# Sliding-window attention on TensorE as dense 128 by 136 score tiles per head, in place of elementwise work on VectorE and the weaving of two token classes

## The chip, the cores and the metric

The kernel runs on one core of a Trainium2 chip. The metric is the time on the device in microseconds, lower is better. The spread of one kernel's runs is small: the kernel before took 1353.09 to 1357.71 us. The mean granted TensorE clock of the profiled run was 0.989 for the kernel before.

The engines go by these names: PE is TensorE (matmuls), PEld its weight loads, DVE is VectorE, ACT is ScalarE, POOL is GpSimd, SP issues the DMAs.

## The reference, cut to what matters

Four blocks in a row, attention, MLP, attention, MLP, over 2048 tokens of width 1024, in bf16. The attention looks back at eight tokens, two apart: token s sees s, s-2, ..., s-14. So even and odd tokens never meet in it, and they form two "classes" of 1024 tokens each. There are 32 heads of 32 dimensions. The MLP mixes tokens: its first product contracts over all 2048 tokens, both classes.

```python
def _A_ref(x, wqkv, wo):              # H = 32, Dh = 32, W = 8, dil = 2
    qkv = ... (x @ wqkv) ...          # B, H, S, Dh each
    off = jnp.arange(W) * dil
    idx = pos[:, None] - off[None, :]
    mask = idx >= 0
    logits = jnp.einsum("bhsd,bhswd->bhsw", q, kg) * scale     # kg = k gathered at idx
    logits = jnp.where(mask[None, None, :, :], logits, -1e9)
    attn = _softmax(logits, axis=-1)
    o = jnp.einsum("bhsw,bhswd->bhsd", attn, vg)
    return (...o...) @ wo

def _B_ref(x, w1, b1, w2, b2):        # F = 3584
    h = _layernorm(x)
    u = _gelu(jnp.einsum("bsd,sf->bdf", h, w1) + b1)
    y = jnp.einsum("bdf,fs->bds", u, w2) + b2
    return y.transpose(...)

x = x + _A_ref(_layernorm(x), A_wqkv, A_wo);  x = x + _B_ref(_layernorm(x), ...)    # twice
```

## The kernel before

Tokens lie on the partitions: partition p holds eight tokens of a class that follow each other. A query and its eight keys then lie on one partition, apart from a halo of seven slots that two DMAs fetch from the partition above. Scores and values are elementwise work of DVE on chunks of eight heads (`QW` is 256), with tree sums over the 32 dimensions; in three chunks the sums run on PE as products with the identity.

```python
def qk(self, ci):                                   # scores of one chunk, on DVE
    ...                                             # three chunks: tree sums by identity matmuls on PE
    for u0 in range(0, W, WB):                      # WB = 2 of the 8 offsets at a time
        nc.vector.tensor_tensor(out=flat, in0=qb, in1=windows(k, u0, WB, [(1, J * QW)]), op=ALU.mult)
        nc.vector.tensor_tensor(out=pr[:, :, 0:16, :], in0=pr[:, :, 0:16, :], in1=pr[:, :, 16:32, :], op=ALU.add)
        nc.vector.tensor_tensor(out=pr[:, :, 0:8, :], in0=pr[:, :, 0:8, :], in1=pr[:, :, 8:16, :], op=ALU.add)
        nc.vector.tensor_tensor(out=St[...], in0=pr[:, :, 0:4, :], in1=pr[:, :, 4:8, :], op=ALU.add)
...
def pv(self, ci):                                   # values, on DVE
    for u in range(W):
        dst = Tv if u else o_q
        nc.vector.tensor_tensor(out=dst[...], in0=v, in1=pw, op=ALU.mult)
        if u:
            nc.vector.tensor_tensor(out=o_q[:], in0=o_q[:], in1=Tv[:], op=ALU.add)
    self.transpose(ci, 0, J)                        # a DMA transpose for the output projection
...
def proj(self, ci, *parts, ...):                    # Q, K or V of a chunk: 256-column matmuls
    for jp in range(J // 2):
        for part in parts:
            ...
            nc.tensor.matmul(ps[:, jj, :], lhsT=self.lhs(c, kt, j), rhs=wts[part][:, kt, :], ...)
            nc.scalar.activation(out=buf[...], in_=ps[...], func=ACT.Identity)      # ACT empties PSUM
            ...                                     # halo DMAs for K and V
```

While DVE works at a chunk, a generator called `weave` hands PE other matmuls, by declared costs of each piece: the output projection of the other class, partial sums of the first MLP product over one class, or the second MLP product of the layer before for the second class.

```python
for unit in chain(lead, last):                      # lead: the attention stream; fill: other matmuls
    ...
    add(unit)
    while t[0] < t[1]:                              # t = [PE time, DVE time] by declared costs
        u = next(fill, None)
        if u is None:
            break
        add(u)
```

## Time and profile before

| what | before |
|---|---|
| time, median | 1355.73 us (later runs beside it: 1355.34) |
| span of the profiled run | 1353.0 us |
| PE busy | 1294.1 us, 96% |
| DVE busy | 772.2 us, 57% |
| ACT busy | 434.4 us, 32% |

The page of the kernel before, its first and fourth parts and three lines of its fifth. In the first, each engine has its busy time, share of the span and number of instructions. In the fourth, shares of the chain of waits that ended last. In the fifth, a group's line, engine and operation, its shapes, its count, then busy us, mean ns of one, and the engine's idle time before it.

```profile
span 1353.0 us, 18269 instructions
...
PE 1294.1 (96%) x7552; PEld 759.6 (56%) x7552; DVE 772.2 (57%) x959; ACT 434.4 (32%) x884; POOL 40.5 (3%) x28
...
PE 59%; DVE 27%; issue 6%; ACT 3%; DMA 2%; POOL 2%; SPq 0%; POOLq 0%; DVEq 0%; ACTq 0%
...
L272 PE MATMUL ps<-wq,hT 128*128 128x256 bf16 x3008 | 351.4, 277 | 21.4 <-ACT v L274 12.9
...
L308 DVE TENSOR_TENSOR T<-q,k 128x4096 bf16<-128x4096 bf16 x52 | 118.6, 2281 | 37.1 <-ACT q L274 23.1
```

The mean of one 256-column matmul is 277 ns, but that is latency: matmuls follow each other faster than they finish. The Trainium skill, "Trainium Kernel Development and Optimization", Performance Expectations, warns of this: it calls matmul busy time a bad metric, because matmuls are pipelined. These matmuls are 277 ns long, but start 109 ns apart. What counts is the cadence, from start to start, and the chain of waits shows it. Here are two pieces of it for the kernel before (start in us, length in us, what):

```profile
228.51 3.49 PE ps L272 x32
...
498.11 6.04 PE pso L559 x28
```

So 32 matmuls of 256 columns take 3.49 us, 0.109 us each, and 28 of 512 columns take 6.04 us, 0.2158 us each (0.1092 and 0.21583 before rounding, which the table uses). With the counts of the groups PE has this dense work:

| PE work before | matmuls | us |
|---|---|---|
| two MLP products, both layers | 3584 of 512 columns | 773.5 |
| output projection | 512 of 512 | 110.5 |
| Q, K, V | 3072 of 256 | 335.4 |
| identity matmuls (tree sums, value sums, residual) | 320 | 48.6 |
| transposes of the first tiles | 64 of 128 | 3.6 |
| sum | | 1271.6 |

The span is 1353.0 us. The first matmul starts at 7.7 us and the last ends 4.4 us before the end. Some 69 us are left.

The view of waits says what PE waited for; these are its largest entries before a matmul (waiter, what it waited for, us in total, times, longest):

```profile
PE ps L272 <- ACT v L274: 12.9, 8, 2.8
...
PE pso L236 <- DVE g L211: 8.2, 2, 7.7
...
PE pso L375 <- DVE T L372: 7.0, 1, 7.0
PE pso L559 <- DMA w<-in_B_w_dram: 6.2, 3, 2.3
```

### The profile page before, as it was taken

What the parts mean: (1) busy time and instruction counts of PE and PEld (TensorE: products, weight loads), DVE (VectorE), ACT (ScalarE), POOL (GpSimd) and SP (SyncE); (2) the same over time, 40 slices, a digit from 0 to 9 for tenths busy, and PEclk for the clock granted to TensorE, in tenths of its full rate; (3) what the DMA queues carried; (4) which work ended last, traced back from release to release, by engine and by line L of the source; (5) the groups of instructions that cost most, each with busy time, mean ns of one, the idle gap of its engine ahead of it and who ended that gap; (6) DMA issues with size and microseconds to landing.
All of it is one profiled execution on the core that took longest, in us unless ns stands there. A gap on an engine that the chain in (4) does not pass through costs nothing.

```text
span 1353.0 us, 18269 instructions
## 1 busy us (share of the span) xinstructions
PE 1294.1 (96%) x7552; PEld 759.6 (56%) x7552; DVE 772.2 (57%) x959; ACT 434.4 (32%) x884; POOL 40.5 (3%) x28
## 2 busy tenths in 40 slices
PE   6989999999999999999998999989799999999998
PEld 5877756754444444459674488665344444444443
DVE  4899999996711433327999649979761033111111
ACT  4377347533122430003333434763222134000000
POOL 2000000000000000000000000100000000000000
PEclk9999999999999999999999999999899999999999
DMA  4458543743452229864477954444245222434431
GB/s 126 149 121 187 139 115 121 191 108 94 133 140 78 74 73 224 223 166 127 138 176 188 233 161 117 140 135 109 71 136 142 64 85 67 119 96 116 137 101 59
DMA packets 290111, 175.18 MB, mean 129 GB/s; under 512 B 66445, under 2 KB 267657, under 8 KB 290026
## 3 DMA queue, kind: packets, MB, share of 16 engines
q1 hardware_dynamic: 289914, 173.98, 48.1%
q8 instruction: 59, 0.97, 0.3%
q14 instruction: 26, 0.21, 0.1%
q0 software_dynamic: 112, 0.01, 0.0%
HBM read 127.94 MB, written 16.78 MB: 107 GB/s over the span
## 4 chain that ended last, share of the span: by engine, by line
PE 59%; DVE 27%; issue 6%; ACT 3%; DMA 2%; POOL 2%; SPq 0%; POOLq 0%; DVEq 0%; ACTq 0%
PE psg L537 13%; PE psg L559 11%; PE pso L559 11%; PE pso L537 8%; DVE Tv L356 6%; PE ps L272 6%; DVE o_q L359 5%; DVE T L308 5%; PE pso L503 5%; PE ps L537 4%; DVE T L310 2%; DVE T L293 1%; POOL L L326 1%; DVE T L312 1%; DVE St L314 1%
## 5 line engine op out<-in xcount | busy, mean ns | idle before, releaser
L272 PE MATMUL ps<-wq,hT 128*128 128x256 bf16 x3008 | 351.4, 277 | 21.4 <-ACT v L274 12.9
L272 PEld LDWEIGHTS <-hT 128*128 128x128 bf16 x3072 | 323.3, 122 | 55.6 <-issue 17.4
L559 PEld LDWEIGHTS <-w 128*128 128x128 bf16 x1792 | 174.9, 98 | 217.3 <-DMA w<-in_B_w_dram 9.3
L537 PEld LDWEIGHTS <-w 128*128 128x128 bf16 x1792 | 175.8, 98 | 212.7 <-issue 4.8
L537 PE MATMUL psg<-h,w 128*128 128x512 bf16 x896 | 211.1, 381 | 0.0
L559 PE MATMUL pso<-g,w 128*128 128x512 bf16 x896 | 199.9, 379 | 6.3 <-DMA w<-in_B_w_dram 6.2
L559 PE MATMUL psg<-g,w 128*128 128x512 bf16 x896 | 198.9, 379 | 0.0
L537 PE MATMUL pso<-h,w 128*128 128x512 bf16 x640 | 151.5, 379 | 1.9 <-ACT h L216 1.9
L308 DVE TENSOR_TENSOR T<-q,k 128x4096 bf16<-128x4096 bf16 x52 | 118.6, 2281 | 37.1 <-ACT q L274 23.1
L503 PE MATMUL pso<-wo,oT 128*128 128x512 bf16 x512 | 118.6, 381 | 3.5 <-DMA oT<-o_q 3.4
L548 DVE TENSOR_TENSOR tmp<-pso,g 128x512 f32<-128x512 f32 x40 | 27.7, 692 | 159.4 <-PE pso L537 159.4
L359 DVE TENSOR_TENSOR o_q<-o_q,Tv 128x2048 bf16<-128x2048 bf16 x91 | 111.2, 1222 | 0.8
L356 DVE TENSOR_TENSOR Tv<-v,Pb 128x2048 bf16<-128x2048 bf16 x91 | 110.8, 1218 | 0.7
L564 DVE SCALAR_TENSOR_TENSOR xo<-psg,b_sb,xs 128x512 bf16<-128x512 f32 x32 | 24.0, 749 | 127.0 <-PE psg L559 127.0
L564 DVE SCALAR_TENSOR_TENSOR xo<-pso,b_sb,xs 128x512 bf16<-128x512 f32 x32 | 24.0, 749 | 120.3 <-PE pso L559 112.4
L503 PEld LDWEIGHTS <-oT 128*128 128x128 bf16 x512 | 50.1, 98 | 63.1 <-DMA oT<-o_q 4.2
L549 ACT ACTIVATE g<-tmp,b_sb 128x512 bf16<-128x512 f32 x80 | 57.7, 721 | 82.1 <-DVE tmp L548 82.1
L310 DVE TENSOR_TENSOR T<-T 128x2048 bf16<-128x2048 bf16 x52 | 63.1, 1214 | 0.4
L274 ACT ACTIVATE k<-ps 128x512 bf16<-128x512 f32 x64 | 38.1, 596 | 69.7 <-PE ps L272 67.7
L178 ACT ACTIVATE ln<-mv,eps 128x1 f32<-128x1 f32 x32 | 9.5, 296 | 152.9 <-DVE mv L187 152.9
L326 POOL TENSOR_SCALAR_AFFINE_SELECT L<-L 1x512 f32<-1x512 f32 x16 | 31.2, 1949 | 910.5 <-DVE L L323 815.7
L537 PE MATMUL ps<-h,w 128*128 128x512 bf16 x256 | 57.9, 379 | 0.0
(89 smaller groups left out, 831.4 us busy)
## 6 DMA issues: line engine op xcount, KB each, us to landing
w<-in_B_w_dram SPq DMA_DIRECT2D x96, 448.0 KB, 4.6
w<-in_B_w_dram SPq DMA_DIRECT2D x56, 512.0 KB, 5.1
wq<-in_A_wqkv_dram SPq DMA_DIRECT2D x47, 512.0 KB, 4.3
wo<-in_A_wo_dram SPq DMA_DIRECT2D x64, 128.0 KB, 2.8
xa<-xn SPq DMA_DIRECT2D x32, 256.0 KB, 2.1
xs<-xa SPq DMA_DIRECT2D x32, 256.0 KB, 3.3
v<-v SPq DMA_DIRECT2D x16, 392.0 KB, 4.9
k<-k SPq DMA_DIRECT2D x15, 392.0 KB, 5.1
```

The source lines that it names most:

```text
L272: nc.tensor.matmul(ps[:, jj, :], lhsT=self.lhs(c, kt, j), rhs=wts[part][:, kt, :], start=(kt == 0), stop=(kt == KD - 1))
L274: nc.scalar.activation(out=buf[:, off + 2 * jp:off + 2 * jp + 2, :].rearrange("p j (d h) -> p j d h", h=HQ), in_=ps[:].rearrange("p j (h d ...
L308: nc.vector.tensor_tensor(out=flat, in0=qb, in1=windows(k, u0, WB, [(1, J * QW)]), op=ALU.mult)
L310: nc.vector.tensor_tensor(out=pr[:, :, 0:16, :], in0=pr[:, :, 0:16, :], in1=pr[:, :, 16:32, :], op=ALU.add)
L326: nc.gpsimd.affine_select(out=L[0:1], in_=L[0:1], compare_op=ALU.is_ge, fill=NEG, base=1 - W, pattern=[[1, W], [1, J], [0, HQ]], channel_m ...
L356: nc.vector.tensor_tensor(out=dst[:].rearrange("p j (d h) -> p j d h", h=HQ), in0=v, in1=pw, op=ALU.mult)
L359: nc.vector.tensor_tensor(out=o_q[:], in0=o_q[:], in1=Tv[:], op=ALU.add)
L503: nc.tensor.matmul(ps[:], lhsT=at_.oT[c][kt // 2][:, j, kt % 2, :], rhs=wo_t[n][kt // 4][:, kt % 4, :], start=(kt == 0), stop=(kt == KD - ...
L537: nc.tensor.matmul(ps[:], lhsT=wt[c][:, j, fl * P:(fl + 1) * P], rhs=h2[c][:, j, dc * 512:(dc + 1) * 512], start=(k == 0), stop=(k == nk - 1))
L549: nc.scalar.activation(out=gs, in_=tmp[:], func=ACT.Gelu_apprx_tanh, bias=b1_sb[:, ft:ft + 1])
L559: nc.tensor.matmul(ps[:], lhsT=w2t[ft // HF][:, ft % HF, c::DIL], rhs=g[ft // GF][:, ft % GF, dc * 512:(dc + 1) * 512], start=(ft == 0), s ...
L564: nc.vector.scalar_tensor_tensor(out=xo[:, dc * 512:(dc + 1) * 512], in0=ps[:], scalar=b2_sb[:, i, c:c + 1], in1=xs[:, dc * 512:(dc + 1) * ...
```

## The change

The intent is to give attention to PE. The heads now lie on the partitions (`qT`, `kT`: four heads of 32 dimensions make 128 rows). For a tile of 128 keys and one head, one matmul computes the scores of these keys against 136 queries (128 and the 8 that follow, since the window reaches seven back in the class). It has 32 rows, so four heads use the four 32-row tiles of the array. ACT takes the exp (with a constant shift, no maximum), DVE multiplies by a band of ones and zeros, and PE multiplies by V, 32 columns a head, so that four heads use the four 32-column tiles. Matmuls with ones give the denominators; Ln and Exp on ACT turn them into reciprocals. No class has to wait for the other, and the weave, the halo copies and the partial MLP sums go. The diff, cut to its core:

```diff
-    def qk(self, ci): ...          # elementwise scores on DVE, 52 products of 4096 elements
-    def softmax(self): ...
-    def pv(self, ci): ...          # 104 products and 91 sums of 2048 elements on DVE
-    def pv_pe(self, ci, bufs): ... # value sums by identity matmuls
-    def weave(lead, fill, then, last): ...
+    def qk_chunk(u, wts, part, n):             # 8 matmuls of 512 columns: Q or K of 4 heads, 512 tokens
+        ...
+        nc.vector.tensor_copy(out=dst[:, lo:lo + 512], in_=ps[:])
+    def scores(u, r):                          # round r: 3, 3 or 2 tiles of 128 keys, 4 heads
+        ss = [s_tile() for _ in range(2)]
+        for t in ts:
+            lo = c * SC + t * P
+            for h in range(HG):
+                hp = slice(h * DH, (h + 1) * DH)
+                nc.tensor.matmul(ss[h // 2][:, h % 2, (t - ts[0]) * KW:(t - ts[0] + 1) * KW],
+                                 lhsT=k[hp, lo:lo + P], rhs=q[hp, lo:lo + KW], start=True, stop=True)
+        for b in range(2):
+            pv = pm[:, 2 * b:2 * b + 2, ts[0]:ts[0] + n, :]
+            nc.scalar.activation(out=..., in_=ss[b][:, :, 0:n * KW], func=ACT.Exp, scale=scale, bias=shift[:])
+            nc.vector.tensor_tensor(out=pv, in0=pv, in1=mk, op=ALU.mult)          # band mask
+    def values(u, b, v, oT):                   # half b: 4 tiles of 128 tokens
+        acc = a_tile()                         # one buffer, 2 x 512 columns in fp32
+        for i in range(-1 if b else 0, hb):
+            for h in range(HG):
+                ... nc.tensor.matmul(acc[hp, 0, ...], lhsT=lhs, rhs=pm[:, h, t, 0:w], ...)
+        for h in range(HG):
+            ... nc.tensor.matmul(acc[hp, 1, :]..., lhsT=ones[:], rhs=pm[:, h, t0:t0 + hb, 0:P], ...)
+        ...                                    # and the 8 columns that reach over: ones again
+        nc.scalar.activation(out=rd[:], in_=acc[:, 1, :], func=ACT.Ln)
+        nc.scalar.activation(out=rd[:], in_=rd[:], func=ACT.Exp, scale=-1.0)
+        nc.vector.tensor_tensor(out=oT[g][:, lo:lo + hb * P], in0=acc[:, 0, :], in1=rd[:], op=ALU.mult)
+    for u in range(NU):                        # 16 units a layer: 4 heads, one class
+        ...                                    # fill: the four projection chunks of the next unit
+        scores(u, 0)
+        fill[0]()
+        if u:
+            values(u - 1, 1, v, oT)
+        scores(u, 1)
+        fill[1]()
+        scores(u, 2)
+        fill[2]()
+        values(u, 0, v, oT)
+        fill[3]()
```

## The prediction

> **What bounds the kernel now.** TensorE. The page's first part gives PE 1294.1 us busy (96% of 1353.0 us), DVE 772.2 (57%), ACT 434.4. PE busy counts latency, so I cost it by cadence. The chain of waits shows 28 matmuls of 512 columns in 6.04 us (0.2158 us each); 128 projection matmuls of 256 columns take 13.96 us (0.109 each). With the groups' counts: MLP 3584 x 0.2158 = 773 us, output projection 512 x 0.2158 = 110, QKV 3072 x 0.109 = 335, identity matmuls and transposes about 52. Sum 1271. So about 82 us are PE slack: the start, and attention, where DVE holds the chain (27% of it; a q*k product takes 2.28 us).
>
> **Removed.** DVE attention: q*k products and tree sums (about 240 us), value products and sums (about 270), softmax pieces (about 100); halo copies; partial first-GEMM sums and their 80 adds; most of the 52 us of identity matmuls.
>
> **Unchanged.** MLP and output projection on PE, 884 us. QKV becomes 1536 matmuls of 512 columns: 331 us, the same. Dense PE work is 1217 us; the rest must fit in 136 us to tie.
>
> **Added**, per unit (4 heads, one class; 32 units). On PE 32 score matmuls of 136 columns on 32-row tiles, 36 value matmuls (mostly 136 columns) and 16 with ones on 32-column tiles. End to end at the cadence above that is near 5.8 us; if four tiles run together, near 1.6. The Trainium skill, "TensorEngine Tiling (Array Packing)", Key Properties, says that tiles execute in parallel and that changing the tiling mode drains the engine; no run shows either. The built order has about 12 mode changes a unit; my guess is 0.1 us each. I take 2.0 us for matmuls plus 1.0 for changes.
>
> ACT per unit: exp of 816 elements x4 and 544 x2, Ln and Exp of 512 x2. From a 512-element copy at 0.59 us and 1024 at 1.01: 0.84, 0.61 and 0.6, together 7.0 us. DVE: band mask (2048 elements 1.22 us, 512 0.42, so 816 about 0.58) 3.2 us, four copies out of PSUM 2.7, two products 1.4: 7.3 us. PE has 6.9 us of projection per unit plus 3, so PE leads, but both score buffers serve each round: the third round waits for the second's two exps behind Ln and Exp. I allow 0.5 us. A unit then takes 10.4 us, against 6.9 of projection.
>
> **Sum.** 1217 dense + about 18 start + 4 tail + 8 stage changes + 32 x 3.3 = 1353. I predict **1350 us, 1305 to 1415**. Faster by over 2%: 0.30; within 2%: 0.40; slower by over 2%: 0.30. The freed DVE time can return at most the 82 us of slack, and the new PE work takes about that back.
>
> **What would show it.** DVE busy falls to 350-430 us, ACT rises to about 420. A middle unit lasts 10 to 11 us. Four score matmuls of different row tiles start within about 60 to 120 ns if tiles overlap, about 230 if not. Chain of waits: nearly all PE, with ACT exp and DVE mask pieces in attention.
>
> **What would make it wrong.** No tile overlap: a unit of 13 to 14 us, above 1440. Near-free mode changes and full overlap: a unit of 8.8, near 1300. Exp, Ln and mask latencies serialising with the single value accumulator: 12 us, 1400. A slow start through twelve DMA transposes: 10 us more.

(One reading in it was taken at one remove: the 13.96 us for 128 projection matmuls is four times the 3.49 us for 32 shown above.)

## The result, and the profile after

| what | before | after |
|---|---|---|
| time, median | 1355.34 us (4 runs) | 1340.16 us (4 runs) |
| ratio | | 0.989 (0.9876 to 0.9904) |
| PE busy | 1294.1 us | 1312.7 us |
| DVE busy | 772.2 us | 428.3 us |
| ACT busy | 434.4 us | 406.7 us |

A ratio here is the mean time of one kernel's runs over that of the other's of the same rounds, so it is not quite the ratio of the medians quoted. The change is 1.1% faster, clear of noise and within 2%. The outputs are right.

The page of the changed kernel, the same parts:

```profile
span 1338.2 us, 19150 instructions
...
PE 1312.7 (98%) x8352; PEld 590.5 (44%) x8352; DVE 428.3 (32%) x774; ACT 406.7 (30%) x622; POOL 3.9 (0%) x13
...
PE 92%; ACT 6%; DMA 1%; issue 0%; DVE 0%; SPq 0%
```

The chain is now 92% PE, and DVE is off it. The groups of the new work, from the view of groups with shapes kept apart:

```profile
L252 ACT ACTIVATE Pm<-s,shift 128x816 bf16<-128x816 f32 x128 | 112.9, 931 | 39.0 <-PE s L248 39.0
...
L255 DVE TENSOR_TENSOR Pm<-Pm,band 128x816 bf16<-128x816 bf16 x128 | 74.3, 581 | 28.8 <-ACT Pm L252 25.0
...
L248 PE MATMUL s<-qT,kT 32*128 32x136 bf16 x1024 | 41.0, 221 | 8.3 <-ACT Pm L252 6.0
```

In the lines of this kernel, L248 is a score matmul, L233 a projection of Q or K, L269 and L273 values, L277 and L285 the matmuls with ones, L252 exp, L255 the mask, L288 and L289 Ln and Exp of the denominators. (In e6 and e8 the lines stand a few further down.) Here is one unit in the middle of the first layer, PE alone, from the timeline of the changed kernel (start us, length us with latency, engine, line, operation, count; in brackets idle time and releaser):

```profile
150.88 0.36 PE L248 MATMUL s<-qT,kT 32*128 32x136 bf16 x12
151.17 1.90 PE L233 MATMUL m<-hT,wqk 128*128 128x512 bf16 x8
153.00 0.19 PE L269 MATMUL acc<-Pm,v 128*32 128x8 bf16 x4
153.04 0.40 PE L273 MATMUL acc<-Pm,v 128*32 128x136 bf16 x16
153.27 0.39 PE L277 MATMUL acc<-Pm,ones 128*32 128x512 bf16 x4
153.48 0.19 PE L285 MATMUL acc<-Pm,ones 128*32 128x32 bf16 x4
153.60 0.36 PE L248 MATMUL s<-qT,kT 32*128 32x136 bf16 x12
153.90 1.90 PE L233 MATMUL m<-hT,wqk 128*128 128x512 bf16 x8
155.88 0.29 PE L248 MATMUL s<-qT,kT 32*128 32x136 bf16 x4
156.11 0.39 PE L233 MATMUL m<-hT,wqk 128*128 128x512 bf16 x1
156.71 0.29 PE L248 MATMUL s<-qT,kT 32*128 32x136 bf16 x4 [0.21 <-ACT Pm L252]
156.94 1.68 PE L233 MATMUL m<-hT,wqk 128*128 128x512 bf16 x7
158.55 0.42 PE L273 MATMUL acc<-Pm,v 128*32 128x136 bf16 x16
158.80 0.39 PE L277 MATMUL acc<-Pm,ones 128*32 128x512 bf16 x4
159.01 0.18 PE L285 MATMUL acc<-Pm,ones 128*32 128x24 bf16 x4
159.13 1.90 PE L233 MATMUL m<-hT,wqk 128*128 128x512 bf16 x8
160.96 0.36 PE L248 MATMUL s<-qT,kT 32*128 32x136 bf16 x12
```

The unit takes 160.96 - 150.88 = 10.08 us. Of these, 32 projection matmuls take 32 x 0.2158 = 6.91 us, so attention costs PE 3.17 us a unit. Reading from start to start shows three kinds of time.

- Matmuls. Twelve scores have a length of 0.36 us, of which one matmul's latency is 0.22 us (the 221 ns above). So twelve start within 0.14 us, about 13 ns apart on average (in the trace's records they come in three groups of four: a group starts within 10 ns, the next some 65 ns later). One tile alone would need near 60 ns for each, as e7 below measures. The tiles do run together.
- Changes of tiling mode. A chunk of eight projection matmuls that starts at 151.17 is through at 151.17 + 8 x 0.2158 = 152.90; the values start at 153.00. Such a gap of 0.10 us comes at each place where nothing is waited for (158.45 to 158.55 and 160.86 to 160.96 too). The order of this unit has eleven changes.
- Waits. From 155.63 to 155.88 the gap is 0.25, and from 156.33 to 156.71 it is 0.38. Less 0.10 each for the change of mode, some 0.43 us a unit are a wait. The bracket shows only 0.21 of it: the profile counts PE as busy for the whole modelled length of the last projection matmul, until 156.50.

What is waited for is in the same unit's timeline with all engines. These are ACT's lines from it:

```profile
153.74 0.60 ACT L288 ACTIVATE rd<-acc 128x512 f32<-128x512 f32 x1 [0.70 <-PE acc L285]
...
154.37 0.63 ACT L289 ACTIVATE rd<-rd 128x512 f32<-128x512 f32 x1
...
154.91 2.96 ACT L252 ACTIVATE Pm<-s,shift 128x816 bf16<-128x816 f32 x4
```

The second round's scores were done at about 153.9, but ACT first computed Ln and Exp for the previous unit's denominators, until 155.0. Only then came the two exps that empty the score buffers, and the third round needs these buffers.

### The profile page after: what moved, and what is told of

Read it like the earlier page. It is cut to its first block, busy times and chain, and to the rows that moved or that the text cites. A ratio compares the mean times of both kernels' runs of the same rounds, so it can differ in the third digit from the quotient of the medians. Undisturbed runs are those within 1.5% of the kernel's fastest.

```text
span 1338.2 us, 19150 instructions
## 1 busy us (share of the span) xinstructions
PE 1312.7 (98%) x8352; PEld 590.5 (44%) x8352; DVE 428.3 (32%) x774; ACT 406.7 (30%) x622; POOL 3.9 (0%) x13
## 4 chain that ended last, share of the span: by engine, by line
PE 92%; ACT 6%; DMA 1%; issue 0%; DVE 0%; SPq 0%
PE s L337 14%; PE s L380 14%; PE m L233 13%; PE m L311 8%; PE m L216 8%; PE m L380 7%; PE m L337 7%; PE acc L337 7%; PE acc L380 7%; ACT Pm L252 3%; PE s L248 1%; PE acc L273 1%; ACT rd L289 1%; ACT rd L288 1%; PE acc L277 1%; DMA x<-in_A_x_dram 1%
## 5 line engine op out<-in xcount | busy, mean ns | idle before, releaser
L233 PE MATMUL m<-hT,wqk 128*128 128x512 bf16 x1024 | 247.0, 381 | 0.0
L337 PE MATMUL s<-h,w 128*128 128x512 bf16 x896 | 202.8, 379 | 0.0
L380 PE MATMUL s<-g,w 128*128 128x512 bf16 x896 | 199.9, 379 | 0.0
L252 ACT ACTIVATE Pm<-s,shift 128x816 bf16<-128x816 f32 (+1 forms) x192 | 152.0, 859 | 39.6 <-PE s L248 39.6
L233 PEld LDWEIGHTS <-wqk 128*128 128x128 bf16 x1024 | 90.3, 98 | 109.2 <-issue 6.6
L216 PE MATMUL m<-wv,hT 128*128 128x512 bf16 x512 | 113.6, 384 | 4.8 <-ACT hT L199 3.7
L311 PE MATMUL m<-wo,oT 128*128 128x512 bf16 x512 | 112.2, 379 | 0.0
L255 DVE TENSOR_TENSOR Pm<-Pm,band 128x816 bf16<-128x816 bf16 (+1 forms) x192 | 99.9, 532 | 29.5 <-ACT Pm L252 25.0
L337 PE MATMUL acc<-h,w 128*128 128x512 bf16 x448 | 103.9, 379 | 0.0
L380 PE MATMUL acc<-g,w 128*128 128x512 bf16 x448 | 100.6, 379 | 0.0
L380 PE MATMUL m<-g,w 128*128 128x512 bf16 x448 | 99.3, 379 | 0.0
L216 PEld LDWEIGHTS <-hT 128*128 128x128 bf16 x512 | 50.3, 99 | 66.8 <-ACT hT L199 4.4
L288 ACT ACTIVATE rd<-acc 128x512 f32<-128x512 f32 x64 | 38.2, 596 | 66.7 <-PE acc L285 66.7
```

The costliest lines, as they stand in the source:

```text
L216: nc.tensor.matmul(ps[:], lhsT=hT[:, kt, cols(c, i)], rhs=wv[n][kt // 4][:, kt % 4, :], start=(kt == 0), stop=(kt == KD - 1))
L233: nc.tensor.matmul(ps[:], lhsT=wts[part][:, kt, (g % 2) * P:(g % 2 + 1) * P], rhs=hT[:, kt, lo:lo + 512], start=(kt == 0), stop=(kt == KD ...
L252: nc.scalar.activation(out=pv.rearrange("p h t k -> p h (t k)"), in_=ss[b][:, :, 0:n * KW], func=ACT.Exp, scale=scale, bias=shift[:])
L255: nc.vector.tensor_tensor(out=pv, in0=pv, in1=mk, op=ALU.mult)
L288: nc.scalar.activation(out=rd[:], in_=acc[:, 1, :], func=ACT.Ln)
L311: nc.tensor.matmul(ps[:], lhsT=oT[g][:, cols(c, i)], rhs=wo[n][g // 4][:, g % 4, :], start=(g == 0), stop=(g == NG - 1))
```

## The experiments

Twelve kernels ran. The table has them in the order of the text below. "Before" is the median of the kernel before in the same call. The changed kernel was not run again in these calls: a difference from its 1340.16 us, or between runs of two calls, carries the drift between calls (the medians of the kernel before went from 1354.86 to 1356.74 us).

| run | what | us | before | ratio (95%) |
|---|---|---|---|---|
| e1_dense_only | after, no attention core (wrong) | 1240.89 | 1354.86 | 0.9155 (0.914 to 0.9171) |
| e2_head_major | after, heads outside | 1345.95 | 1354.86 | 0.9935 (0.992 to 0.995) |
| e7_one_row_tile | after, all scores on one row tile (wrong) | 1368.99 | 1355.55 | 1.0101 (1.0087 to 1.0115) |
| e6_split_values | after, four more mode changes a unit | 1357.87 | 1355.55 | 1.002 (1.0007 to 1.0033) |
| e4_no_mask | after, no band mask (wrong) | 1339.77 | 1355.55 | 0.9882 (0.9865 to 0.9899) |
| e5_no_reciprocal | after, no Ln and Exp (wrong) | 1321.58 | 1354.86 | 0.9752 (0.9737 to 0.9766) |
| e3_values_first | after, one call moved | 1323.87 | 1354.86 | 0.9769 (0.9755 to 0.9784) |
| e8_fewer_changes | e3 and one mode change less | 1315.57 | 1355.55 | 0.9704 (0.9689 to 0.9718) |
| e9_loads_first | e8 and another order of loads | 1313.91 | 1355.58 | 0.9694 (0.968 to 0.9708) |
| b1_no_sums | before, no value sums (wrong) | 1342.05 | 1356.74 | 0.9899 (0.9884 to 0.9914) |
| b2_light_dve | before, DVE attention mostly cut (wrong) | 1339.47 | 1356.74 | 0.9883 (0.9866 to 0.99) |
| b5_light_v_on_dve | b2 with V's copy on DVE (wrong) | 1326.49 | 1355.58 | 0.9788 (0.9771 to 0.9805) |

The theory to test (A in the expectations): in both kernels PE is the bound. The change trades PE work and gaps of the old attention, about 115 us in all, for about 100 us of new PE work. The main rival: DVE was the bound, and the gain should have been large but is lost again to the exp, mask and accumulator latencies of the new chain. Two further points of A could be wrong in themselves: whether tiles really overlap, and what a change of mode costs.

### e1_dense_only: what the attention core costs

```diff
-            scores(u, 0)
+            copy_only(u)               # two DVE copies qT -> oT, so that the rest runs on
             fill[0]()
-            if u:
-                values(u - 1, 1, v, oT)
-            scores(u, 1)
...
-            scores(u, 2)
...
-            values(u, 0, v, oT)
```

> The changed kernel with its attention core taken out (no score, value or ones matmuls, no exp, mask, Ln; two plain DVE copies per unit write oT; wrong result on purpose). Theory A (everything added sits on TensorE as matmuls, mode changes and a short wait, 3.1 us a unit, and all else in the kernel is dense): 1240 us, give or take 4, which is 1217 of dense matmuls plus 17.4 start, 4 tail and about 1. Rival B (TensorE is held by the exp and mask latencies of ACT and DVE in more than the attention units, for instance at the stage changes or in the first matmuls): below 1230, or above 1250 if the dense part itself has hidden waits.

Measured: 1240.89 us, as theory A said. The attention core costs 1340.16 - 1240.89 = 99.3 us, 3.1 us for each of 32 units. Everything else is dense: 1217.4 us of full-array matmuls, the first one at 6.8 us, 4.1 us after the last, and the 11.0 us that are left of the 1239.3 us span. Of these 11.0, by start-to-start reckoning, 9.9 us lie in the first 50 us, and some 3 of them are not gaps but matmuls at half cadence (V's first start 0.43 us apart, at a granted clock of 0.50). Hardly anything is to be had at the changes of stage.

### e2_head_major: another order of the same matmuls

```diff
-        for t in ts:
-            lo = c * SC + t * P
-            for h in range(HG):
+        for h in range(HG):
+            for t in ts:
+                lo = c * SC + t * P
```

and the same in the loop of the value matmuls.

> The changed kernel with the same score and value matmuls in another order: head outside, token tile inside, so that neighbours in the queue share one 32-row or 32-column tile. Theory A (the four tiles really run together because neighbours are on different tiles: twelve scores cost about 0.17 us, not 0.68): score and value matmuls then cost near 57 ns each and not 14, so 32 x 43 ns + 36 x 40 ns = about 2.8 us a unit, 80 to 90 us in all: 1420 to 1430 us. Rival (the matmuls are short because they have few rows or few columns, or because TensorE reorders them itself): within 5 us of 1340.

Measured: 1345.95 us, 5.8 us more. Theory A's expectation of 80 to 90 us failed, and the rival's (that PE reorders, within about 5 us) held. The program's order was as meant: three score matmuls of head 0, three of head 1, and so on; in the values five of head 0 (one of L269, four of L273), then five of head 1, and the ones (L277) after all twenty. A rebuild of the kernel shows that the compiled program keeps this order. PE's timeline of this kernel shows what became of it:

```profile
154.79 0.18 PE L269 MATMUL acc<-Pm,v 128*32 128x8 bf16 x1
154.83 0.22 PE L273 MATMUL acc<-Pm,v 128*32 128x136 bf16 x1
154.83 0.18 PE L269 MATMUL acc<-Pm,v 128*32 128x8 bf16 x1
...
154.93 0.33 PE L273 MATMUL acc<-Pm,v 128*32 128x136 bf16 x9
155.06 0.38 PE L277 MATMUL acc<-Pm,ones 128*32 128x512 bf16 x1
155.08 0.23 PE L273 MATMUL acc<-Pm,v 128*32 128x136 bf16 x2
...
155.52 0.38 PE L248 MATMUL s<-qT,kT 32*128 32x136 bf16 x12
```

The L269 of the second head starts at 154.83, when only one of the four L273 queued before it has started. A matmul with ones starts at 155.06, ahead of value matmuls at 155.08 that stand before it in the program. So, in this trace, the tiles each go on with their own matmuls, and a matmul for one tile passes queued ones for another. Order within groups such as these is hardly a lever for overlap. The Trainium skill, "TensorE: Matmul & The Clock Gate", The mechanism, says the opposite: matmuls are "pc-monotone in start AND end". For starts, this trace differs, and the measurement decides; ends are modelled in the profile and say nothing. The few us more lie mostly in the values: from 154.79 to 155.52 they take 0.73 us, where the changed kernel took 0.60 (153.00 to 153.60), and the other half takes 0.61 and not 0.58; a round of twelve scores takes 0.31 and not 0.29.

One thing besides the order of heads differs. The order of the built program is made by a scheduler at build time, and here it does not split the third round around a projection matmul: two changes of mode a unit fewer, but a longer wait (14.3 us in the view of waits for scores behind exps, against 6.0). The two nearly cancel: from the end of the chunk before, the third round takes 1.14 us without its projection matmul, against 1.10. So the order of heads itself costs some 6 us.

### e7_one_row_tile: take the overlap away

```diff
-                                 lhsT=k[hp, lo:lo + P], rhs=q[hp, lo:lo + KW], start=True, stop=True)
+                                 lhsT=k[0:DH, lo:lo + P], rhs=q[0:DH, lo:lo + KW], start=True, stop=True)
```

> The changed kernel with all score matmuls reading the first 32 rows of K and Q, so that all fall on one row tile (heads 1 to 3 of a group get head 0's scores; wrong result on purpose). Their number and shapes stay. The head-major run cost only 6 us, and its trace shows matmuls of later heads starting before queued ones of earlier heads; so order did not take the overlap away, and this run does. Theory A (four row tiles run at once): 32 matmuls at 57 ns and not 14 ns, 1.4 us a unit, 44 us in all, of which some is hidden where TensorE waits for exps: 1375 to 1385 us. Rival (a 32-row matmul is short in itself and nothing overlaps): within 5 us of 1340.

Measured: 1368.99 us, 28.8 us more; the direction is theory A's, the size a little under its range. The timeline of this kernel, two lines next to each other:

```profile
168.21 0.88 PE L248 MATMUL s<-qT,kT 32*128 32x136 bf16 x12
169.02 1.90 PE L233 MATMUL m<-hT,wqk 128*128 128x512 bf16 x8
```

Twelve scores now start over 0.88 - 0.22 = 0.66 us, 60 ns apart, and the next chunk comes 0.81 us after the first of them and not 0.29 us. That is 0.52 us for each of the two rounds of twelve. The third round's two halves take 0.34 us each and not 0.23, which adds 0.22: 1.26 us in all. But the wait of 0.43 us before and in that round is gone, since the exps now have time (each gap there is the 0.10 of the change of mode). So a unit should be 0.83 us longer, and it is: 10.92 us (third rounds start at 163.18 and 174.10). The term that my range missed is this wait, hidden more fully than I had allowed. So overlap is real and worth about 29 us for the scores alone. On one tile, a 32-row matmul takes what its columns take: 0.109 us for 256 columns would make 58 ns for 136 (an estimate), and 60 was measured.

### e6_split_values: four more changes of tiling mode

```diff
         for ... value matmuls ...
+        if between:
+            between()                  # four of the eight matmuls of a projection chunk
         for h in range(HG):
             ... matmuls with ones ...
...
-            fill[0]()
-            if u:
-                values(u - 1, 1, v, oT)
+            if u and not last:
+                halves[0]()
+                values(u - 1, 1, v, oT, halves[1])
...
-            values(u, 0, v, oT)
-            fill[3]()
+            values(u, 0, v, oT, halves[6])
+            halves[7]()
```

> The changed kernel with half a projection chunk between the value matmuls and the ones matmuls, twice a unit; the same instructions, four more changes of the tiling mode a unit (120 or so in a layer pair). Theory A (each change between full-array matmuls and tiles costs about 0.1 us of TensorE, as the gaps of the trace at such places suggest): 4 x 0.1 x 30 = 12 us more, 1350 to 1354 us. Rival (the gaps are waits for data, and a change of mode itself is free): 1338 to 1342.

Measured: 1357.87 us, 17.7 us more, 0.59 us for each of 30 units. That is theory A's direction, but 4 us above its range. The same instructions run; only their order differs. PE's timeline of this kernel, the first half of a unit's values split in two:

```profile
152.48 0.42 PE L276 MATMUL acc<-Pm,v 128*32 128x136 bf16 x16
152.83 1.04 PE L233 MATMUL m<-hT,wqk 128*128 128x512 bf16 x4
153.79 0.40 PE L282 MATMUL acc<-Pm,ones 128*32 128x512 bf16 x4
...
154.14 1.04 PE L233 MATMUL m<-hT,wqk 128*128 128x512 bf16 x4
...
155.40 1.04 PE L233 MATMUL m<-hT,wqk 128*128 128x512 bf16 x4
156.55 0.19 PE L272 MATMUL acc<-Pm,v 128*32 128x8 bf16 x4
```

From 152.48 to 154.14 are 1.66 us, of which four projection matmuls are 0.86. The split half takes 0.80 us, where the unsplit one took 159.13 - 158.55 = 0.58. Two more changes cost 0.22 us, 0.11 each. The other half comes to the same. The rest of a unit's growth is mostly a new wait of 0.19 us (with it, this unit comes to 10.71 us, 0.63 more than 10.08): the four matmuls from 155.40 are through at 156.26, the values start at 156.55, and 0.10 of that is the change of mode. It comes at the values' first matmul, so the likely cause is the single value accumulator, which the previous half now gives up later and the next half wants earlier. The trace fits: DVE's product that empties the accumulator runs from 155.82 to 156.50. No run tested it. The Trainium skill, "TensorEngine Tiling (Array Packing)", Key Properties, says that a change of tiling mode drains the engine. A change costs time: 0.10 to 0.12 us. That the cost is a drain, the runs do not show.

### e4_no_mask: is DVE's part on the critical path?

```diff
-            mk = band[:].unsqueeze(1).unsqueeze(1).to_broadcast([P, 2, n, KW])
-            nc.vector.tensor_tensor(out=pv, in0=pv, in1=mk, op=ALU.mult)
```

> The changed kernel without the band mask on DVE (wrong result on purpose): 3.2 us of DVE a unit less, 100 us in all. Theory A (DVE is off the critical path): 1335 to 1340 us. Rival (the chain exp, mask, values holds TensorE): 1325 or lower.

Measured: 1339.77 us, no difference (DVE busy falls from 428.3 to 338.7 us). DVE's mask costs no time here.

### e5_no_reciprocal and e3_values_first: what makes the wait

```diff
-        nc.scalar.activation(out=rd[:], in_=acc[:, 1, :], func=ACT.Ln)
-        nc.scalar.activation(out=rd[:], in_=rd[:], func=ACT.Exp, scale=-1.0)
-        nc.vector.tensor_tensor(out=oT[...], in0=acc[:, 0, :], in1=rd[:], op=ALU.mult)
+        nc.vector.tensor_copy(out=oT[...], in_=acc[:, 0, :])
```

> The changed kernel without Ln and Exp of the denominators (oT is a plain copy of the unnormalised sums; wrong result on purpose). ACT has 1.23 us less twice a unit. Theory A (Ln and Exp ahead of the second round's exps make TensorE's wait): the wait before the third round goes, 1325 to 1330 us, about as the run with the values moved. Rival (the two exps of 0.93 us and their latencies alone, against one chunk of 1.73 us, make the wait): half of it or more stays, 1333 to 1340.

Measured: 1321.58 us, 18.6 us less. The other run leaves the work as it is and moves one call:

```diff
             scores(u, 0)
-            fill[0]()
             if u:
                 values(u - 1, 1, v, oT)
+            fill[0]()
             scores(u, 1)
```

> The changed kernel with one call moved: the second half of the previous unit's values comes before the first projection chunk, not after it, so that its Ln and Exp go through ACT while TensorE still has a chunk to do, and the second round's exps are no longer held behind them. Theory A (TensorE's wait of about 0.45 us a unit before the third round of scores comes from Ln and Exp standing ahead of two exps in ACT's queue): the wait goes, 30 units x 0.45 = 13 us, 1326 to 1329 us. Rival (the wait only moves: the single value accumulator is not free that early, because the DVE product that empties it ends 0.3 us after the scores begin): 1335 to 1340.

Measured: 1323.87 us, 16.3 us less, with right outputs. That is 0.977 of the kernel before, faster by more than 2%. Both runs say that the wait is made by Ln and Exp standing ahead of the exps in ACT's queue. Both gained a little more than expected. A part of that is seen in the built order of both: the scheduler no longer splits the third round around a projection matmul, so two changes of mode, some 0.2 us, go as well as the wait. e3's unit is 9.49 us long (its first scores start at 157.31 us, the next unit's at 166.80). Its third round, from PE's timeline of this kernel:

```profile
162.21 0.41 PE L248 MATMUL s<-qT,kT 32*128 32x136 bf16 x8
162.56 1.90 PE L233 MATMUL m<-hT,wqk 128*128 128x512 bf16 x8
```

These eight scores still take 0.35 us (162.21 to 162.56), a little long for eight.

### e8_fewer_changes: the third round next to the values

```diff
             scores(u, 1)
             fill[1]()
-            scores(u, 2)
-            fill[2]()
-            values(u, 0, v, oT)
+            halves[4]()                # first half of chunk 2
+            scores(u, 2)
+            values(u, 0, v, oT)
+            halves[5]()                # second half; the last unit keeps e3's order
             fill[3]()
```

> The kernel with the values moved first (1323.9 us), and the third round of scores put directly before the first half of the values, with half of the projection chunk before both and half behind: eight changes of mode a unit where that kernel has nine. Theory A: 0.1 us a unit less, 3 us in all, 1319 to 1322 us, if no new wait comes up. Rival (masks of the second round are not done when the values start, or the accumulator is not free for the next half): 1324 to 1335.

Measured: 1315.57 us, 8.3 us less than e3 (their ratios to the kernel before do not overlap), more than the 3 us that one change of mode explains, and below theory A's range. PE's timeline of this kernel shows the rest:

```profile
160.74 0.30 PE L251 MATMUL s<-qT,kT 32*128 32x136 bf16 x8
160.97 0.42 PE L276 MATMUL acc<-Pm,v 128*32 128x136 bf16 x16
```

The eight scores now take 0.23 us and not 0.35. So e3 still had a wait of about 0.12 us inside the third round, which twelve projection matmuls before it, in place of eight, cover. A unit is 9.22 us here, and attention costs PE 2.31 us.

### e9_loads_first: the start

```diff
-            fill_wv(wv, 0)
             next(pro[2])
             next(pro[3])
+            fill_wv(wv, 0)
             fill_wv(wv, 1)
```

> The kernel with values first and fewer changes of mode (1315.6 us), with the loads of the third and fourth input tile put before those of the V weights. Theory A (the 3 to 4 us that TensorE waits at 14 to 17 us is for these two tiles, which land late because the weights go first): 1.5 to 3 us less, 1312 to 1314 us. Rival (the weights then land later by as much): 1315 to 1317.

Measured: 1313.91 us against 1315.57; the intervals of the two ratios overlap, so the times alone do not part them. PE's timeline has the seventeenth V matmul at 20.72 us here (first line) and at 22.95 us in e8 (second), which fits theory A's 1.5 to 3 us, though 0.58 us of it is there at the first matmul already (6.96 against 7.54 us):

```profile
20.72 9.45 PE L216 MATMUL m<-wv,hT 128*128 128x512 bf16 x42 [1.81 <-ACT hT L199]
```

```profile
22.95 7.30 PE L216 MATMUL m<-wv,hT 128*128 128x512 bf16 x33 [0.60 <-ACT hT L199]
```

With nothing lost, it is the fastest version: 0.969 of the kernel before, 1.96% under the changed kernel by the medians (1313.91 to 1340.16).

### b1_no_sums and b2_light_dve: was DVE the bound before?

```diff
                 nc.vector.tensor_tensor(out=dst[...], in0=v, in1=pw, op=ALU.mult)
                 if u:
-                    nc.vector.tensor_tensor(out=o_q[:], in0=o_q[:], in1=Tv[:], op=ALU.add)
                     yield 0.0, 1.16        # declared cost kept: the weave's order stays
```

> The kernel before, without the 91 sums of value products on DVE (111 us of DVE work; wrong result on purpose), all else kept. Theory A: the gain is capped by the slack that DVE makes in attention, about 60 us, and only part of the chunks wait for DVE; 1305 to 1335 us. Rival (DVE bound): the full 111 us, near 1245.

Measured: 1342.05 us, 14.7 us less, for 111 us of DVE work removed. Less than expected (1305 to 1335), and nowhere near the rival's 111. The second run removes much more: the q*k products are cut to an eighth, their first two sums go, and only one of eight value products is left. Its diff is of the same kind, again with the declared costs kept.

> The kernel before, with most of its DVE attention taken out and its order of instructions kept: q*k products cut to an eighth and their first two tree sums dropped in the chunks that use DVE alone, value products only for one of eight offsets and no sums of them (wrong result on purpose). DVE loses about 420 of 772 us. Theory A (the kernel before is bound by TensorE, with at most 82 us of slack beside 1271 us of dense matmuls, of which the start and the tail take about 20): 1285 to 1310 us. Rival (DVE is the bound, 27% of the chain of waits, 365 us): below 1200. Second rival (the slack is made by the weave's order and DMA, not by DVE): above 1330.

Measured: 1339.47 us, 17.3 us less. DVE busy fell from 772.2 to 392.9 us. The main rival is out: 379 us of DVE work less give 17. But theory A's 1285 to 1310 failed as well, and the second rival (above 1330: the gaps are not DVE's making) held. I had put the gaps of the kernel before down to DVE because DVE had 27% of the chain of waits. Most of these gaps stay when DVE has half as much to do. Nor are the 17 us all waits for DVE: the mean granted clock of b2's runs was 0.993 to 0.996 and of b1's 0.994 to 0.998, that of the kernel before beside them 0.987 to 0.994. If PE loses time in proportion, that is about 5 us of b2's gain and 7 of b1's, by my estimate.

### b5_light_v_on_dve: whose gaps are they?

```diff
-                    nc.scalar.activation(out=buf[...], in_=ps[...], func=ACT.Identity)
+                    if part == 2:
+                        nc.vector.tensor_copy(out=bo, in_=bi_)      # V, by the idle DVE
+                    else:
+                        nc.scalar.activation(out=bo, in_=bi_, func=ACT.Identity)
```

> The light-DVE variant of the kernel before (1339.5 us), with the copy of V out of PSUM moved from ACT to the now idle DVE (wrong result on purpose, as there). With DVE cut, 54 us of gaps between matmuls were left, of which the waits view gives 9.5 us in ten waits to a projection matmul that waits for ACT to empty its V buffer. Theory A (those gaps are ACT's in-order queue: the copy stands behind ACT work that is itself waiting): 1329 to 1333 us. Rival (one wait gives way to another in the same chain of projection, copy, halo DMA, q*k): 1336 to 1342.

Measured: 1326.49 us, 13.0 us less than b2, more than the 9.5 us of waits that pointed to it. The view of waits of b2 has the first of these lines, the view of b5 the second:

```profile
PE ps L273 <- ACT v L275: 9.5, 10, 2.2
```

```profile
PE ps L273 <- DVE v L278: 4.0, 8, 0.8
```

So part of the old gaps came from V's copies queueing behind other work of ACT. The entry itself fell by only 5.5 us; where the other 7 or 8 came from is not shown. Some 44 us over the floor (1327.0 of span, less 1271.6, 7.7 and 4.0) are left even then. The view of waits spreads them over the start, weight loads, transposes and ACT; I did not take them apart further, and this stays open.

## Why the prediction was right or wrong

The time was within the range and near its middle: 1340.16 us against 1350 (1305 to 1415), and the class "within 2%" was the likeliest of the three. Point by point:

- **PE bounds both kernels, and 1217 us of it are common: right.** The run without attention took 1240.89 us, where dense work, start and tail alone gave 1240.
- **The cost of attention on PE: right in sum, less so in its parts.** I took 3.3 us a unit in the sum (10.4 in the text for a unit with 6.9 of projection, 3.5); the trace has 3.17, and the run without attention gives 99.3 us in all against 105.6. Its parts: overlap was assumed and is real (13 ns a score on four tiles, 60 ns on one); a change of mode was guessed at 0.1 us and costs 0.10 to 0.12; the wait was put at 0.5 us and is about 0.43, in the place named, the third round behind Ln and Exp. With eleven changes (12 were expected), 1.1 to 1.3 us go to them, where I took 1.0, and 1.4 to 1.6 are left for the matmuls, where I took 2.0. So errors of opposite sign met, and that the sum is this close is partly luck. Nor did four scores start within 60 to 120 ns, as I wrote, but within 10.
- **Start 18, tail 4: right** (8.1 us to the first matmul and about 10 us lost after it, some 3 of these by half cadence; 4.0 us at the end). **Stage changes 8: too much**, they cost under 1 us. This and the 6 us of attention are the whole difference between the sum of 1353 and the result.
- **Busy times**: DVE was to fall to 350 to 430 us and is at 428.3; ACT was to be about 420 and is at 406.7; "rises" was a slip, since it stood at 434.4 before. The chain is nearly all PE (92%) with ACT (6%), as expected, but without mask pieces of DVE (0%). An exp of 816 elements took 0.93 us and not the 0.84 that a straight line through two copies gave; Ln and Exp were as expected. Masks at 0.58 us were exact.
- **"Attention, where DVE holds the chain": wrong.** The 82 us of slack were there, but DVE made little of them. With 379 us of DVE work taken out, 17.3 us came back, some 5 of them by the granted clock. A share of the chain of waits says where the last-ending chain passed, not what time would be saved. The waits that stopped PE, by the view of waits, were many and small: ACT's copies (moving V's gave 13 us in b5, with DVE's work cut), the start, weight loads. About 11 us more are the stretches at half cadence that begin in or soon after such waits; the changed kernel's only one, from 14.8 to 21.7 us, is at its start.

So the change's 15 us are the difference of two larger sums, and each term has a number. By cadence, PE loses 54.2 us of other work (1271.6 - 1217.4: 48.6 of identity matmuls, 3.9 on Q, K, V, 1.8 of transposes). Gaps and half-cadence stretches outside the tiled work fall from 69.3 us to about 10. Against these 114 us stand 99 us of tiled attention. The start and tail are within 1 us of what they were. That leaves the 15 us.

Where the large freed amount on DVE went is answered by b2 and e4: it was off the critical path before, and what DVE does now is off it too. And the rival, latency in the new chain, is right only for 0.43 us a unit, with some 0.2 more for the two changes of mode of the split third round; moving one call gave back 16 us.

## What to carry to other kernels

Before moving work off an engine, ask what the bound engine stands still for, gap by gap; a rival engine's share of busy time, or of the chain of waits, is no measure of the gain, and the cheap test is to delete its work and keep the order. Price TensorE by start to start, and with tiles in play count three things per unit of work: the overlapped matmuls, the changes of tiling mode, and the waits. Look at the granted clock by stretch, too: matmuls at half cadence are no wait, and no view of waits shows them. Work on an engine that takes its queue in order, as ACT did here, should be placed where the next thing behind it is not what the bound engine waits for; here that was one moved call, worth about as much as the whole rewrite (16 us against 15).

## What the Trainium skill lacked or had wrong

- "TensorE: Matmul & The Clock Gate", The mechanism, says that matmuls start in program order with no reordering. In e2 matmuls of later heads start before queued matmuls of earlier heads on another tile: an L269 of the second head at 154.83 us, when only one of the four L273 queued before it had started, and a matmul with ones at 155.06 ahead of value matmuls at 155.08. Another order of the same matmuls cost 5.8 us, where starts in program order would have cost 80 to 90 by my estimate.
- "TensorEngine Tiling (Array Packing)", Key Properties, says that a change of tiling mode drains the engine, but gives no cost. Here it is 0.10 to 0.12 us a change: e6, with four more a unit, took 17.7 us more, of which by the trace about 0.45 us for each of 30 units are the four changes.
